# Attention tiles two at a time between the first layer's products, a later first weight step in slab 8, later residual sums

## The chip, the cores and the metric

The kernel runs on one core of a Trainium2 chip. The time is the device time of one execution in microseconds (us), the median of several runs. The profile is that of one execution.

## What is computed

A chain of three layers over 4608 rows (8 batches of 576) of width 512, all in float32:

```python
# 1. attention in chunks of 64 rows, 8 heads of 64
scores = scale * np.matmul(q_c, k_c.transpose(0, 1, 2, 4, 3))
attn = np.exp(scores - np.max(scores, axis=-1, keepdims=True))
attn = attn / (np.sum(attn, axis=-1, keepdims=True) + 1e-09)
x = np.matmul(attn, v_c)          # then heads side by side: 4608 x 512
# 2. first layer, 512 -> 2048 -> 512, with a residual
xn = (x - mu) / np.sqrt(var + 1e-06) * g_ln
x = x + np.maximum(xn @ w_ch1, 0.0) @ w_ch2
# 3. second layer, 512 -> 1024 -> 512, with a convolution of three taps as a gate
h = np.maximum(x @ w_in, 0.0)
return (h * sigmoid(conv(h, conv_w))) @ w_out
```

## The kernel before

Rows go in 36 attention tiles T of 128 rows (two chunks of 64) and in 9 slabs p of 512 rows (tiles 4p to 4p+3). Every large matmul is made of three matmuls (`mm3`, lines 113 to 115) on high and low parts of both operands; ScalarE makes the high part by a cast and VectorE the low part by a subtraction. PSUM is one tile, `banks`, of eight banks.

**Start.** A string, `START`, lists steps by letter and number. For the weights `w_ch1`, a block of four 128x512 pieces: `W` load, `a` (ScalarE), `t`, `m`, `n` (VectorE) turn raw bits into float32, `g` (ScalarE) scales, `s` (VectorE) makes sums, `h` (ScalarE) and `l` (VectorE) make the two parts. The number is that of a piece (0 to 15), for `h` and `l` that of an operand of the products (0 to 27). The letters of attention are below. What stands behind the `|` is run slot by slot in slab 0.

**First layer, first half.** `xn @ w_ch1` is done by the seven products of a fast 2x2 block scheme. A *slot* is one product, 12 matmuls of 128x256 (`product(p, G, n)`). A slab has 4 groups G of 7 slots s, so slot number 28p + 7G + s. `SLOTS` gives the product n of each s, and a lag of one group for two of them. Products 1, 6, 7 and 4 of a group pile up in one bank (4 or 5 by G), and ScalarE copies the running sum out (`u1`, `u6`, `u7`, `u4`, lines 605 and 614) before the next is added. Products 5 and 3 pile up in another bank and product 2 has its own; VectorE adds them to the copies (`plus`, line 159), and SyncE's queue stores the sum in `hd`. At G = 3 the operands of the next slab are made (`both`: a cast on ScalarE into `xc`, line 502, a subtraction on VectorE, line 156).

**Attention, put between slots.** `session(t, tv)` puts the work of tile tv behind slots t to t+4, together with the first half of the next tile, ts = tv+1:
- `V` (TensorE, line 380): 16 matmuls on 64x64 of the array, weights times values, of tv; `S` (same line): 16 such for the scores of ts. Each is two records in the trace (x32).
- `M` (VectorE, 396 and 397): maximum over scores; `X` (VectorE, 434): divide; `L`: loads of q, k, v for the tile after next.
- `E` (ScalarE, 406): 8 exponentials of a tile, in two halves; `R` (VectorE): reciprocals; `B`, `x` (VectorE): normalization of rows.
- `P` (TensorE, 420), `T` (TensorE, 462): four transposes each, of the exponentials of ts and of the rows of tv; `C` and `e` (ScalarE, 426 and 468): copies out of them, to `pt` (which the next `V` reads) and `bst` (from which the next slab's operands come).

Attention uses banks 0 and 1 for `S` and `V`, 0 for `P`, 3 for `T`.

**Slab 8.** It has no sessions. At slot (G, s) = (0, 5) the pool of attention is given back, and loads follow in SyncE's queue: three of `hr` (512 KB of `hd` each) and two raw pieces of `w_ch2` (`wd`). `cv_step` moves the preparation of `w_ch2` one step on: `h` of one piece, `a` of another on ScalarE, `m` and `l` on VectorE, one more load. ScalarE runs its queue in order, so an `a` whose load is out holds the copies behind it.

**First layer, second half.** `Down`: for each slab 16 blocks f of 12 matmuls of 128x512, summed in four banks (0 to 3 and 4 to 7 by turns). `split` makes a block's operands one block ahead: `hh` on ScalarE (685), `hl` on VectorE (686). After a slab's last block, `finish` adds the four sums to the rows of x (`xr`, four additions on VectorE, line 159).

**Second layer.** `Gate` and `outtile`; the change doesn't touch them.

Each engine takes its instructions in the order of the program text, with waits on semaphores between engines.

Of the kernel before, what the change touches and what calls it, by code (L numbers as in the profile page):

```python
# [23 lines left out]
h7 B2 e1 B3 h6 u1 l7 v1 y3 l8 z3 s4 e3 y2 s6 z2 s5 e2 l6 h11 j0 u2 j1 u3  # L24
s7 u5 v3 u7 h10 l11 j2 l10 u6 v2 h12 v6 j3 l12 u4 v5 h13 v4 l13 v7
|
S4 M4 E4 a8 t8 a10 t10 m8 n8
/ g8 a9 t9 m10 n10
/ g10 a11 a12 t11 t12 m9 R4 P4
/ C4 a14 n9 t14 g9 m12  # L30
/ h14 n12 m11 g12 n11 a13
/ l14 t13 g11 m14 h15
/ n14 s8 g14 l15 a15
/ h16 t15 s9 m13 l16 n13
/ s10 g13 s11 h21 h17
# [9 lines left out]
def attn_moe_moe2(  # L45
# [30 lines left out]
    N0, _, D, _, HP = q0.shape[:5]  # L76
    NTILE = N0 + q.shape[0]
# [4 lines left out]
    NS = NT // 512  # L82
# [75 lines left out]
    def plus(out, a, b):  # L158
        nc.vector.tensor_tensor(out=out, in0=a, in1=b, op=ALU.add)  # L159
# [182 lines left out]
    class Attention:  # L342
# [13 lines left out]
        def tile(self, shape, tag, bufs):  # L356
            return self.p.tile(shape, F32, tag=tag, bufs=bufs, name=tag)

        def L(self, T):
            for nm, to in (("q", self.q), ("k", self.k)):  # L360
                t = self.tile([128, HP * 2 * 64], "r" + nm, 2)
                if T < N0:
                    src = (q0 if nm == "q" else k0)[T].rearrange("c d e j s -> e d c (j s)")
                    for e in range(2):
                        nc.sync.dma_start(
                            out=t[half(e)].rearrange("p (c n) -> p c n", c=2), in_=src[e]
                        )
                    to[T] = t.rearrange("p (c j s) -> p j c s", c=2, s=64)
                else:
                    src = (q if nm == "q" else k)[T - N0]  # L370
                    nc.sync.dma_start(out=t, in_=src.rearrange("e p j c s -> (e p) (j c s)"))
                    to[T] = t.rearrange("p (j c s) -> p j c s", c=2, s=64)
            t = self.tile([128, HP * 2 * 64], "rv", 3)
            nc.sync.dma_start(out=t, in_=v[T].rearrange("e s j c d -> (e s) (j c d)"))
            self.v[T] = t.rearrange("p (j c d) -> p j c d", c=2, d=64)
# [22 lines left out]

        def E(self, T, js=range(4)):
            if T not in self.pp:  # L400
                self.sm[T] = self.tile([128, 2, HP], "sm", 3)
# [116 lines left out]
    with tc.manual_schedule():  # L518
# [4 lines left out]
        at = Attention()  # L523
# [15 lines left out]
        def one(step):  # L539
            kind, i = step[0], int(step[1:])  # L540
            if kind in "atmng":
                getattr(blocks[i // 4], kind)(i % 4)
            elif kind == "W":
                blocks[i // 4].W(i % 4, nc.sync)
            elif kind == "w":
                blocks[i // 4].W(i % 4, nc.scalar)
            elif kind == "s":
                blocks[i // 4].s(i % 4)
            elif kind in "hl":
                getattr(blocks[i // 7], kind)(i % 7)  # L550
            elif kind in "juv":
                getattr(slabs[0], kind)(i)
            elif kind == "S":
                at.S(i, (4, 6, 0, 4, 0)[i])
            elif kind == "V":
                at.V(i, (4, 6, 0, 4)[i])
            elif kind == "P":
                at.P(i, 0 if i > 3 else 2)
# [20 lines left out]
        def product(p, G, n):  # L579


            to = {1: 4 + G % 2, 6: 4 + G % 2, 7: 4 + G % 2, 4: 4 + G % 2, 5: 6 + G % 2, 3: 6 + G % 2, 2: 2}[n]
            x = slabs[p].xc[n]
            for i in range(2):
                f = 2 * G + i
# [10 lines left out]
            def flat(t):  # L596
                return t.rearrange("p a n -> p (a n)")
# [8 lines left out]
            if n == 7:  # L606

                t = tops.pop((p, G, 7))
                plus(flat(t), bank[6 + G % 2], flat(t))
                store(3, t)  # L610
            if n == 4:

# [11 lines left out]
                plus(flat(t), bank[to], flat(t))  # L624
                store(1, t)

        SLOTS = ((1, 0), (5, 0), (4, 1), (6, 0), (3, 1), (2, 0), (7, 0))
        events = {}

        def on(t, fn):  # L630
            events.setdefault(t, []).append(fn)

        def session(t, tv):

            ts = tv + 1 if tv + 1 < NTILE else None

            def begin():
                at.V(tv)
                if ts is not None:
                    at.S(ts)  # L640
                    at.M(ts)
                at.X(tv)
                if tv + 2 < NTILE:
                    at.L(tv + 2)

            on(t, begin)
            if ts is not None:
                on(t + 1, lambda: at.E(ts, (0, 1)))
                on(t + 2, lambda: at.E(ts, (2, 3)))
            on(t + 1, lambda: at.B(tv))  # L650
            on(t + 2, lambda: at.x(tv))

            if tv % 4 == 3:
                on(t + 3, lambda: (at.T(tv), at.e(tv)))
            if ts is not None:
                on(t + 4, lambda: (at.R(ts), at.P(ts)))
            if tv % 4 != 3:
                on(t + 4, lambda: at.T(tv))
            if ts is not None:
                on(t + 4, lambda: at.C(ts))  # L660
            if tv % 4 != 3:
                on(t + 4, lambda: at.e(tv))

        for tv in range(4, NTILE):

            t = 28 * (tv // 4 - 1) + 7 * (tv % 4 - 1) + 1
            session({4: 5, 5: 9, 6: 13, 7: 17}.get(tv, t), tv)

        class Down:

# [30 lines left out]
        for p in range(NS + 1):  # L701
            if p + 1 < NS:
                slabs[p + 1] = Slab(p + 1)
            for G in range(4):
                for s, (n, lag) in enumerate(SLOTS):
# [15 lines left out]
                    if p == NS - 1:  # L721
# [9 lines left out]
                        elif (G, s) == (2, 5):  # L731
                            tags = [f"w0{kk}{i}" for kk in range(2) for i in range(7)]
                            for f, tag in zip(F_ORDER[EARLY:], tags):
                                add_w2(f, lambda: wa_p, tag)
                            cv_load(NF1)
                        elif (0, 5) < (G, s) < (2, 5) and s % 2 == 0 or (G, s) in ((3, 1), (3, 3), (3, 5)):
                            cv_step()
                        if (G, s) == (3, 4):
                            parts = down.split(0)
# [51 lines left out]
        todo = [(p, f) for p in range(NS) for f in F_ORDER]  # L791
        downs = {0: down}
        xrs = {}
        for n, (p, f) in enumerate(todo):
            hh, hl = parts

# [7 lines left out]
                parts = downs[todo[n + 1][0]].split(todo[n + 1][1])  # L804
            if p == 0 and n % 4 < 3 or n % 2:
                cv_step()
            if f == 4:
                xrs[p] = residual(downs[p])
            if late and f >= 8:
                late.pop(0)()  # L810
            downs[p].down(f, hh, hl)
            if f == NF1 - 1:
                finish(downs[p], xrs[p])
            if (p, f) == (0, 15):
                cv_rest()
                load_cw()
# [195 lines left out]
```

## Time and profile before

| | |
|---|---|
| median of 3 runs | 1308.42 us (1308.25 to 1308.7) |
| the profiled execution | 1309.48 us, of which the span of its instructions is 1307.5 us |
| TensorE busy | 1249.2 us, 96% |
| VectorE, ScalarE busy | 748.9 us (57%), 614.8 us (47%) |

Times in the rows below are us from the span's start. TensorE's rows overlap, since a matmul's record lasts until its result is out; the pace of TensorE is the distance from start to start. The granted clock of TensorE (PEclk) is a share of 2.4 GHz: 1.00, or 0.50, which is 1.2 GHz, or a mean of both.

### The profile page before, as it was taken

To read this page: it belongs to the slowest core of one execution; us is meant where nothing else is said; L and a number is where in the kernel's file an instruction comes from. 1 tells how busy PE (TensorE), PEld (TensorE's weight loads), DVE (VectorE), ACT (ScalarE), POOL (GpSimd) and SP (SyncE) were. 2 spreads that over 40 slices of the span, in tenths; PEclk is the share of its full clock that TensorE was granted. 3 is DMA by queue.
4 is the path that set the end of the run, shared out by engine and by line. 5 is a ranking of instruction groups with operands and counts; after the bars stand their busy time and mean duration, and the time that the engine had idled before them with its cause. 6 is when DMAs were issued, how large, how long until landed. Compare 5 with 4: busy or idle time off the path is not lost.

```text
span 1307.5 us, 23314 instructions
## 1 busy us (share of the span) xinstructions
PE 1249.2 (96%) x9096; PEld 1087.0 (83%) x9096; DVE 748.9 (57%) x1430; ACT 614.8 (47%) x1510; POOL 76.2 (6%) x172
## 2 busy tenths in 40 slices
PE   5559999999999989999999999999999999999998
PEld 4459999999999978787788888888788888888887
DVE  7986565566556557667733443343876655565540
ACT  6765555556556435343322222222765555455541
POOL 0000000000000000000000000000121211111100
PEclk6689999999999989999999999999999999999999
DMA  9534555555455358486444355432111111101001
GB/s 267 169 106 170 186 172 168 188 186 177 168 183 191 114 205 298 146 296 211 145 153 161 128 178 178 161 130 81 33 57 58 43 37 57 57 28 53 25 25 49
DMA packets 127021, 177.70 MB, mean 136 GB/s; under 512 B 12736, under 2 KB 72128, under 8 KB 126912
## 3 DMA queue, kind: packets, MB, share of 16 engines
q1 hardware_dynamic: 126912, 176.22, 40.3%
q8 instruction: 71, 1.16, 0.4%
q14 instruction: 38, 0.31, 0.1%
HBM read 110.13 MB, written 66.06 MB: 135 GB/s over the span
## 4 chain that ended last, share of the span: by engine, by line
PE 85%; DVE 6%; ACT 4%; DMA 3%; issue 1%; SPq 1%; POOL 0%; DVEq 0%; ACTq 0%; POOLq 0%
PE banks L113 27%; PE banks L114 26%; PE banks L115 26%; PE banks L380 3%; PE banks L462 1%; PE banks L420 1%; DMA w<-in_moe_w_ch_dram 1%; DVE w L156 1%; ACT pp L406 1%; DMA wd<-in_moe_w_ch_dram 1%; DVE w L151 0%; DMA x2d<-x2T 0%; ACT w L335 0%; DVE xr L159 0%; DVE w L145 0%
## 5 line engine op out<-in xcount | busy, mean ns | idle before, releaser
L113 PE MATMUL banks<-xc,w 128*128 128x256 f32 x1008 | 290.4, 288 | 7.6 <-ACT u L605 7.1
L114 PE MATMUL banks<-xc,w 128*128 128x256 f32 x1008 | 283.2, 281 | 4.5 <-DVE xc L156 4.5
L115 PE MATMUL banks<-xc,w 128*128 128x256 f32 x1008 | 282.9, 281 | 0.0
L685 ACT ACTIVATE hh<-hr 128x512 fp32r<-128x512 f32 x144 | 91.1, 632 | 262.0 <-PE banks L115 261.8
L686 DVE SCALAR_TENSOR_TENSOR hl<-hr,hh 128x512 fp32r<-128x512 f32 x144 | 99.2, 690 | 192.1 <-ACT hh L685 189.9
L113 PEld LDWEIGHTS banks<-xc,w 128*128 128x128 f32 x1008 | 193.3, 192 | 10.5 <-ACT u L605 7.5
L114 PEld LDWEIGHTS banks<-xc,w 128*128 128x128 f32 x1008 | 193.6, 192 | 4.7 <-DVE xc L156 4.7
L115 PEld LDWEIGHTS banks<-xc,w 128*128 128x128 f32 x1008 | 193.3, 192 | 0.0
L113 PE MATMUL banks<-w,hl 128*128 128x512 f32 x396 | 154.7, 391 | 0.0
L114 PE MATMUL banks<-w,hh 128*128 128x512 f32 x396 | 154.1, 389 | 0.0
L115 PE MATMUL banks<-w,hh 128*128 128x512 f32 x396 | 154.1, 389 | 0.0
L896 DVE SCALAR_TENSOR_TENSOR cv<-hb,cw_sb,cv 128x510 f32<-128x510 f32 (+31 forms) x256 | 117.2, 512 | 0.6
L113 PE MATMUL banks<-xb,w 128*128 128x512 f32 x288 | 113.5, 394 | 1.8 <-ACT hb L881 1.4
L114 PE MATMUL banks<-xb,w 128*128 128x512 f32 x288 | 113.0, 393 | 0.0
L115 PE MATMUL banks<-xb,w 128*128 128x512 f32 x288 | 112.9, 392 | 0.0
L159 DVE TENSOR_TENSOR u<-banks,u 128x512 f32<-128x512 f32 x108 | 73.6, 688 | 56.2 <-ACT u L605 31.1
L406 ACT ACTIVATE pp<-banks,mx 128x64 f32<-128x64 f32 x288 | 87.8, 336 | 8.1 <-DVE mx L397 5.4
L605 ACT COPY u<-banks 128x512 f32<-128x512 f32 x108 | 64.0, 593 | 56.7 <-PE banks L115 54.1
L113 PEld LDWEIGHTS banks<-w,hl 128*128 128x128 f32 x396 | 74.3, 188 | 17.4 <-DVE hl L686 2.1
L115 PEld LDWEIGHTS banks<-w,hh 128*128 128x128 f32 x396 | 74.3, 188 | 15.6
L114 PEld LDWEIGHTS banks<-w,hh 128*128 128x128 f32 x396 | 74.3, 188 | 15.2
L883 POOL COPY hal<-hb 128x2 f32<-128x2 f32 x64 | 41.8, 652 | 736.6 <-ACT hb L881 736.6
(106 smaller groups left out, 2197.8 us busy)
## 6 DMA issues: line engine op xcount, KB each, us to landing
hd<-u SPq DMA_DIRECT2D x144, 256.0 KB, 2.9
hr<-hd SPq DMA_DIRECT2D x72, 512.0 KB, 3.8
w<-in_moe_w_ch_dram SPq DMA_DIRECT2D x27, 512.0 KB, 6.8
rv<-in_v_dram SPq DMA_DIRECT2D x36, 256.0 KB, 3.7
xd<-x SPq DMA_DIRECT2D x36, 256.0 KB, 2.0
xr<-xd SPq DMA_DIRECT2D x36, 256.0 KB, 4.3
x2d<-x2T SPq DMA_DIRECT2D x36, 256.0 KB, 2.0
x2r<-x2d SPq DMA_DIRECT2D x36, 256.0 KB, 4.0
```

The lines of the kernel that those rows point to most:

```text
L113: nc.tensor.matmul(ps, ll, rh, start=first, stop=False, **kw)
L114: nc.tensor.matmul(ps, lh, rl, start=False, stop=False, **kw)
L115: nc.tensor.matmul(ps, lh, rh, start=False, stop=last, **kw)
L156: nc.vector.tensor_tensor(out=out, in0=a, in1=b, op=ALU.subtract)
L159: nc.vector.tensor_tensor(out=out, in0=a, in1=b, op=ALU.add)
L380: nc.tensor.matmul(ps[half(c), e, j, :], lt[half(e), j, c, :], rt[half(e), j, c, :], start=True, stop=True,)
L406: nc.scalar.activation(out=pp[:, j, e, :], in_=self.both[T][:, e, j, :], func=AF.Exp, scale=SCALE, bias=mx[:, e, j:j + 1], accum_out=sm[:, ...
L605: nc.scalar.copy(flat(t), bank[to])
L685: nc.scalar.activation(out=self.hh, in_=t, func=AF.Relu)
L686: nc.vector.scalar_tensor_tensor(out=self.hl, in0=t, scalar=0.0, in1=self.hh.bitcast(F32), op0=ALU.max, op1=ALU.subtract,)
L883: nc.gpsimd.tensor_copy(out=hal[:, f, :], in_=hb[:, 512:514])
L896: nc.vector.scalar_tensor_tensor(out=cv[:, a:e], in0=hb[:, a + tap:e + tap], scalar=cw_sb[:, tap, f:f + 1], in1=cv[:, a:e], op0=ALU.mult, ...
```

## The change

A session now takes two tiles (tv, tv+1), each with banks of its own (0 and 1, or 2 and 3: `side`). Behind slot t stand `V` `V` `S` `S`, and behind slot t+6 (`turn`) `P` `P` `T` `T`. A slab has two sessions, at its slots 0 and 13, in place of four. Products 5 and 3 use bank 6 in all groups, product 2 uses bank 7, and `SLOTS` takes the products in another order. In slab 0, the sessions of tiles 4 to 7 are at slots 7 and 14 in place of 5, 9, 13 and 17. In slab 8, `cv_step` is not run at (0, 6), so the first is that of (1, 0). `finish` runs one block later, behind the next `split`.

```diff
-S4 M4 E4 a8 t8 a10 t10 m8 n8
-/ g8 a9 t9 m10 n10
-/ g10 a11 a12 t11 t12 m9 R4 P4
...
+S4 S5 M4 M5 E4 L6 L7 a8 t8 a10 t10 m8 n8
+/ E5 g8 a9 t9 m10 n10
+/ g10 a11 a12 t11 t12 m9
...
-            to = {1: 4 + G % 2, 6: 4 + G % 2, 7: 4 + G % 2, 4: 4 + G % 2, 5: 6 + G % 2, 3: 6 + G % 2, 2: 2}[n]
+            to = {1: 4 + G % 2, 6: 4 + G % 2, 7: 4 + G % 2, 4: 4 + G % 2, 5: 6, 3: 6, 2: 7}[n]
...
-        SLOTS = ((1, 0), (5, 0), (4, 1), (6, 0), (3, 1), (2, 0), (7, 0))
+        SLOTS = ((1, 0), (2, 0), (3, 1), (6, 0), (4, 1), (5, 0), (7, 0))
...
-            ts = tv + 1 if tv + 1 < NTILE else None
+            tvs = tv, tv + 1
+            tss = [T for T in (tv + 2, tv + 3) if T < NTILE]
+            side = lambda T: T % 2 * 2
 
             def begin():
-                at.V(tv)
-                if ts is not None:
-                    at.S(ts)
-                    at.M(ts)
-                at.X(tv)
-                if tv + 2 < NTILE:
-                    at.L(tv + 2)
+                for T in tvs:
+                    at.V(T, side(T))
+                for T in tss:
+                    at.S(T, side(T))
+                for i in range(2):
+                    if tss:
+                        at.M(tss[i])
+                    at.X(tvs[i])
...
+            def turn():
+                for T in tss:
+                    at.R(T)
+                    at.P(T, side(T))
+                for T in tvs:
+                    at.T(T, side(T) + 1)
+                for i in range(2):
+                    at.e(tvs[i])
+                    if tss:
+                        at.C(tss[i])
 
             on(t, begin)
...
+            for i, T in enumerate(tss):
+                on(t + 1 + 2 * i, lambda T=T: at.E(T, (0, 1)))
+                on(t + 2 + 2 * i, lambda T=T: at.E(T, (2, 3)))
+            for i, T in enumerate(tvs):
+                on(t + 1 + i, lambda T=T: at.B(T))
+                on(t + 3 + i, lambda T=T: at.x(T))
+            on(t + 6, turn)
...
-        for tv in range(4, NTILE):
+        for tv in range(4, NTILE, 2):
...
-            t = 28 * (tv // 4 - 1) + 7 * (tv % 4 - 1) + 1
-            session({4: 5, 5: 9, 6: 13, 7: 17}.get(tv, t), tv)
+            t = 28 * (tv // 4 - 1) + (13 if tv % 4 else 0)
+            session({4: 7, 6: 14}.get(tv, t), tv)
...
-                        elif (0, 5) < (G, s) < (2, 5) and s % 2 == 0 or (G, s) in ((3, 1), (3, 3), (3, 5)):
+                        elif (0, 6) < (G, s) < (2, 5) and s % 2 == 0 or (G, s) in ((3, 1), (3, 3), (3, 5)):
...
+            if ended is not None:
+                finish(downs[ended], xrs[ended])
+                ended = None
...
             downs[p].down(f, hh, hl)
             if f == NF1 - 1:
-                finish(downs[p], xrs[p])
+                ended = p
```

**TensorE at a session** in slab 1 (`rv,pt` is `V`, `rk,rq` is `S`; the rows around are products). Before:

```order
L115 MATMUL banks<-xc,w_679 128x256
L380 MATMUL banks<-rv,pt 64x64 x16
L380 MATMUL banks<-rk,rq 64x64 x16
L113 MATMUL banks<-xc,w_931 128x256
L114 MATMUL banks<-xc,w_931 128x256
```

The same place with the change:

```order
L115 MATMUL banks<-xc,w_620 128x256
L384 MATMUL banks<-rv,pt 64x64 x32
L384 MATMUL banks<-rk,rq 64x64 x32
L113 MATMUL banks<-xc,w_340 128x256
L114 MATMUL banks<-xc,w_340 128x256
```

Each group has doubled, and there are half as many groups.

**ScalarE at a session** at the turn of two slabs (`pp` exponentials, `u` copies of running sums, `xc` casts for the next slab, `bst` and `pt` the copies `e` and `C`). Before, for one tile:

```order
L605 COPY u1_4332<-banks_171 128x512
L502 CAST xc_4337<-bst_3768 128x512
L502 CAST xc_4353<-t1_4334 128x512
L614 COPY u4_4412<-banks_171 128x512
L406 ACTIVATE pp_4416,sm_4415<-banks_171,mx_4388 128x64 x4
L605 COPY u6_4440<-banks_171 128x512
L502 CAST xc_4442<-bst_3768 128x512
L406 ACTIVATE pp_4416,sm_4415<-banks_171,mx_4388 128x64 x4
L502 CAST xc_4479<-bst_3768 128x512
L426 COPY pt_4493<-banks_171 128x512
```

With the change, for two tiles at slot 0 of a slab:

```order
L611 COPY u1_3769<-banks_171 128x512
L410 ACTIVATE pp_3874,sm_3873<-banks_171,mx_3835 128x64 x4
L506 CAST xc_3900<-bst_3281 128x512
L410 ACTIVATE pp_3874,sm_3873<-banks_171,mx_3835 128x64 x4
L611 COPY u6_3926<-banks_171 128x512
L410 ACTIVATE pp_3929,sm_3928<-banks_171,mx_3841 128x64 x4
L620 COPY u4_3948<-banks_171 128x512
L506 CAST xc_3951<-bst_3281 128x512
L410 ACTIVATE pp_3929,sm_3928<-banks_171,mx_3841 128x64 x4
L611 COPY u7_3984<-banks_171 128x512
L472 COPY bst_4008<-banks_171 128x4x128
L430 COPY pt_4010<-banks_171 128x512
```

Sixteen exponentials stand between the copies where eight stood.

**ScalarE in slab 8** (`cy<-wd` is `a` of a piece of `w_ch2`, which waits for its load). Before:

```order
L605 COPY u7_6686<-banks_171 128x512
L133 ACTIVATE cy_6690<-wd0_6670 128x512
L605 COPY u1_6706<-banks_171 128x512
L133 ACTIVATE cy_6708<-wd1_6672 128x512
L614 COPY u4_6739<-banks_171 128x512
```

With the change:

```order
L611 COPY u7_6686<-banks_171 128x512
L611 COPY u1_6702<-banks_171 128x512
L133 ACTIVATE cy_6704<-wd0_6670 128x512
L133 ACTIVATE cy_6736<-wd1_6672 128x512
L611 COPY u6_6755<-banks_171 128x512
L620 COPY u4_6769<-banks_171 128x512
```

The copy `u1` has moved ahead of the first piece; `u6` is the first one behind the pieces, and two pieces stand ahead of it.

## Rows read from the trace of the kernel before

**Rows 1.** Waits of TensorE, whole span: for whom, us in total, times, longest.
```profile
PE banks L380 <- ACT pt L426: 14.5, 6, 5.7
PE banks L113 <- ACT u L605: 7.1, 2, 6.5
PE banks L113 <- DVE hl L686: 3.4, 3, 1.4
```
**Rows 2.** Stretches: length; busy PE, PEld, DVE, ACT, POOL; PEclk, DMA, GB/s.
```profile
65.50:104.80 39.30, 26.04 (x335) 24.48 (x330) 30.86 (x61) 23.04 (x68) 1.94 (x2) 0.78 0.36 115
127.00:450.00 323.00, 322.94 (x4219) 317.03 (x4218) 188.83 (x398) 178.09 (x627) 14.81 (x27) 1.00 0.51 174
450.00:506.00 56.00, 48.41 (x407) 47.78 (x406) 29.69 (x50) 23.96 (x43) 0.00 (x0) 0.94 0.64 229
```
**Rows 3.** Order of time, TensorE at a session: start, us, engine, line, operands, count.
```profile
224.47 0.28 PE L115 MATMUL banks<-xc,w 128*128 128x256 f32 x1
224.68 0.69 PE L380 MATMUL banks<-rv,pt 64*64 64x64 f32 x32
225.19 0.65 PE L380 MATMUL banks<-rk,rq 64*64 64x64 f32 x32
...
226.11 0.28 PE L115 MATMUL banks<-xc,w 128*128 128x256 f32 x1
```
**Rows 4.** Order of time, TensorE at the last session, which has V alone.
```profile
437.00 0.28 PE L115 MATMUL banks<-xc,w 128*128 128x256 f32 x1
437.21 0.69 PE L380 MATMUL banks<-rv,pt 64*64 64x64 f32 x32
...
438.17 0.28 PE L115 MATMUL banks<-xc,w 128*128 128x256 f32 x1
```
**Rows 5.** Order of time, TensorE: transposes P and T between products.
```profile
231.22 0.28 PE L115 MATMUL banks<-xc,w 128*128 128x256 f32 x1
231.33 0.60 PE L420 MATMUL banks<-ident,pp 128*128 128x128 f32 x4
231.77 0.60 PE L462 MATMUL banks<-ident,xn 128*128 128x128 f32 x4
...
232.32 0.28 PE L114 MATMUL banks<-xc,w 128*128 128x256 f32 x1
```
**Rows 6.** Order of time, ScalarE: exponentials and a copy of a running sum.
```profile
229.33 0.33 ACT L406 ACTIVATE pp<-banks,mx 128x64 f32<-128x64 f32 x1
229.53 0.22 ACT L406 ACTIVATION_READ_ACCUMULATOR pp<-banks,mx 128x1 f32 x1
229.62 0.60 ACT L605 COPY u<-banks 128x512 f32<-128x512 f32 x1
230.09 0.36 ACT L406 ACTIVATE pp<-banks,mx 128x64 f32<-128x64 f32 x1
```
**Rows 7.** Order of time, VectorE: M and X of a session.
```profile
225.91 0.69 DVE L396 TENSOR_REDUCE mx<-banks 128x8 f32<-128x512 f32 x1 [1.93 <-PE banks L380]
226.71 0.69 DVE L434 TENSOR_TENSOR x<-banks,sm 128x512 f32<-128x512 f32 x1
```
**Rows 8.** Waits of VectorE between 65.5 and 104.8 us.
```profile
DVE mx L396 <- PE banks L380: 5.2, 2, 3.5
DVE w L156 <- ACT w L335: 2.5, 4, 0.7
```
**Rows 9.** Order of time, TensorE: slot 14 of slab 0, and slot 27.
```profile
99.60 0.58 PE L113 MATMUL banks<-xc,w 128*128 128x256 f32 x1
...
125.45 0.37 PE L113 MATMUL banks<-xc,w 128*128 128x256 f32 x1
```
**Rows 10.** Order of time, slab 8: SyncE's queue, ScalarE, and TensorE behind it.
```profile
466.35 1.19 SPq L124 DMA_DIRECT2D wd<-in_moe_w_ch_dram  x2
...
473.88 0.69 ACT L133 ACTIVATE cy<-wd 128x512 f32<-128x512 f32 x1 [8.71 <-DMA wd<-in_moe_w_ch_dram]
...
475.10 0.58 PE L113 MATMUL banks<-xc,w 128*128 128x256 f32 x1 [6.46 <-ACT u L605]
```

More of the change, by code (lines that the diff above doesn't have):

```diff
@@ L26 @@
 |
-S4 M4 E4 a8 t8 a10 t10 m8 n8
-/ g8 a9 t9 m10 n10
-/ g10 a11 a12 t11 t12 m9 R4 P4
-/ C4 a14 n9 t14 g9 m12
-/ h14 n12 m11 g12 n11 a13
-/ l14 t13 g11 m14 h15
+S4 S5 M4 M5 E4 L6 L7 a8 t8 a10 t10 m8 n8
+/ E5 g8 a9 t9 m10 n10
+/ g10 a11 a12 t11 t12 m9
+/ a14 n9 t14 g9 m12
+/ R4 P4 C4 h14 n12 m11 g12 n11 a13
+/ R5 P5 C5 l14 t13 g11 m14 h15
 / n14 s8 g14 l15 a15
@@ L357, in tile, with L @@
             return self.p.tile(shape, F32, tag=tag, bufs=bufs, name=tag)
-        def L(self, T):
+        def L(self, T, late=False):
             for nm, to in (("q", self.q), ("k", self.k)):
@@ L372, in L, with Lv @@
                     to[T] = t.rearrange("p (j c s) -> p j c s", c=2, s=64)
+            if not late:
+                self.Lv(T)
+        def Lv(self, T):
             t = self.tile([128, HP * 2 * 64], "rv", 3)
@@ L400, in E @@
             if T not in self.pp:
-                self.sm[T] = self.tile([128, 2, HP], "sm", 3)
+                self.sm[T] = self.tile([128, 2, HP], "sm", 4)
                 self.pp[T] = self.tile([128, HP, 2, 64], "pp", 2)
@@ L553, in one @@
             elif kind == "S":
-                at.S(i, (4, 6, 0, 4, 0)[i])
+                at.S(i, (4, 6, 0, 4, 0, 2)[i])
             elif kind == "V":
@@ L557, in one @@
             elif kind == "P":
-                at.P(i, 0 if i > 3 else 2)
+                at.P(i, i % 2 * 2 if i > 3 else 2)
+            elif kind == "L":
+                at.L(i, late=i > 5)
             elif kind in "y":
@@ L608, in product @@
                 t = tops.pop((p, G, 7))
-                plus(flat(t), bank[6 + G % 2], flat(t))
+                plus(flat(t), bank[6], flat(t))
                 store(3, t)
@@ L633, in session @@
         def session(t, tv):
-            ts = tv + 1 if tv + 1 < NTILE else None
+            tvs = tv, tv + 1
+            tss = [T for T in (tv + 2, tv + 3) if T < NTILE]
+            side = lambda T: T % 2 * 2
             def begin():
-                at.V(tv)
-                if ts is not None:
-                    at.S(ts)
-                    at.M(ts)
-                at.X(tv)
-                if tv + 2 < NTILE:
-                    at.L(tv + 2)
-            on(t, begin)
-            if ts is not None:
-                on(t + 1, lambda: at.E(ts, (0, 1)))
-                on(t + 2, lambda: at.E(ts, (2, 3)))
@@ L650, in session @@
[L650 to L662, printed above, removed]
-        for tv in range(4, NTILE):
-            t = 28 * (tv // 4 - 1) + 7 * (tv % 4 - 1) + 1
-            session({4: 5, 5: 9, 6: 13, 7: 17}.get(tv, t), tv)
+                for T in tvs:
+                    at.V(T, side(T))
@@ new lines, in begin @@
+                for T in tss:
[5 more added lines that the diff above has]
+                for T in tss:
+                    if T + 2 < NTILE:
+                        at.L(T + 2, late=True)
+                for T in tss:
+                    at.Lv(T)
+            def turn():
+                for T in tss:
+                    at.R(T)
[6 more added lines that the diff above has]
+                        at.C(tss[i])
@@ L806, in attn_moe_moe2 @@
                 cv_step()
+            if ended is not None:
+                finish(downs[ended], xrs[ended])
+                ended = None
             if f == 4:
@@ L830, in attn_moe_moe2 @@
         cv_rest()
+        finish(downs[NS - 1], xrs[NS - 1])
         for fn in late:
```

## The prediction

> **What bounds the kernel now.** I read the page first: TensorE is busy for 1249.2 of 1307.5 us, so a gain must come either out of its 58 us of idle time or out of work that it does. Then its waits [rows 1]: 14.5 us for `pt`, the copy that `V` reads, 7.1 us for a copy `u` of a running sum, of which 6.5 are one wait, and 3.4 us in three waits for `hl`. Then stretches [rows 2]: in the steady part (127 to 450 us) TensorE has no idle time worth a word, VectorE and ScalarE are busy 58% and 55%, and the granted clock is 1.00. So there only less work on TensorE shortens it. In slab 0 (65.5 to 104.8 us) VectorE is the busiest, 30.9 of 39.3 us, and TensorE is granted 0.78. From 450 to 506 us 7.6 us are idle and 0.94 is granted.
>
> **Term 1: half as many groups of 64x64 matmuls.** The pace of products: from the third matmul of a run at 226.11 to its 48th at 231.22 [rows 3, 5] are 45 steps, 0.1136 us each, so a slot is 1.36 us. Around `V S`, from the last product (224.47) to the third one behind (226.11), 1.64 us pass; three steps of these are 0.34, so `V S` costs 1.30 us [rows 3]. Around `V` alone it is 1.17 - 0.34 = 0.83 us [rows 4]. `S` by itself is then worth 0.47, `V` taken as equal, and the remaining 0.36 us are paid for each entry into such a group. `V V S S` should cost 0.36 + 4 x 0.47 = 2.24 us where two groups cost 2.60. From slot 28 on there are 27 groups before (26 `V S`, one `V`) and 14 with the change: 13 x 0.36 = 4.7 us. Tile 8's `V` and `T` move from slab 0 into this stretch and cost 0.47 + 0.44 there, so 3.8 us stay. Transposes pay no entry: from 231.22 to 232.32 less two steps are 0.87, and one set is 0.44 from start to start [rows 5], so that `P P T T` is no cheaper than twice `P T`. Ends: 0 less the 0.9 if the entry belongs to each tile's banks and not to the group, and 5.
>
> On that entry the Trainium skill has a rule: TensorEngine Tiling (Array Packing), Key Properties, says that a change of tiling mode drains the engine, and TensorE: Matmul & The Clock Gate, step 4 (drain) of its step-by-step part, puts a drain at some 128 cycles, 0.05 us at 2.4 GHz. By my estimate from these pages two changes make 0.11 us an entry and 1.4 us in all in place of 4.7; the rows show three times as much, and the sum keeps to the rows.
>
> **Term 1's cover: ScalarE and VectorE in a session of two tiles.** I follow the tighter one, at slot 0 of a slab, from the start of that slot's product. It ends at 1.4, `V V S S` at 3.6, and slots 1 to 6 end at 5.0, 6.4, 7.7, 9.1, 10.4, 11.8. The first scores are out at 3.1; `M` takes 0.80, so exponentials start at 4.0. They follow each other by 0.29 us, and a copy takes 0.47 of the queue [rows 6]. ScalarE: four to 5.2; a cast that must wait for the product of slot 2 (6.5), to 7.0; four to 8.2; `u6` to 8.7; four to 9.9; `u4` to 10.4; a cast to 10.9; four to 12.1. The last transposes of the second tile are due at 12.6: 0.5 us to spare. VectorE: `M X M X` (0.80 and 0.69 each) [rows 7] to 6.1, `B` to 7.2, the additions of products 2 and 3 to 8.4; product 5 shares bank 6 and needs the latter at 9.1: 0.7 us to spare. Product 6 needs `u1`, 7 needs `u6`, and each stands two slots behind its copy. In the session at slot 13 no casts fall in. So the steady part gets no new wait, on a thin cover: without it each of 13 sessions would wait.
>
> **Term 2: the start, slots 0 to 27.** VectorE's chain from `n12` to the last weight step `l27` ends at 104.8 us, with 7.7 us of waits in it [rows 8], 5.2 of them for scores: `M6` and `M7` stand behind `V5` and `V6`, which wait for `C5` and `C6` in ScalarE's queue. With sessions at 7 and 14 both copies have several slots. The new chain lacks `M5`, `X6` and one addition (0.8 + 0.7 + 0.6) and has one more pair of reciprocals (0.4), so 29.2 us of work for 30.9; it begins 0.7 later, since one addition now comes in slot 1. Of the waits I keep 2.3 (one for `u7`, whose product waits for `u6` behind `E5` on ScalarE, and those of `l24`, `l26`, `l27` for their casts) and 0.5 of small gaps. The chain then ends at 65.5 + 0.7 + 29.2 + 2.8 = 98.2. On ScalarE `h24`, some 5 us before that end, stands ahead of `h25`, `u7`, `e4`, `C6`, `e5`, `C7`: seven steps of 0.5 us to 96.7. `V7 S8 S9` follow (1.6 us with the way out), so slot 15 starts at 98.3; before it started at 99.60 + 12 x 0.213 = 102.2 (1.2 GHz) [rows 9]. From there to slot 28 the new order has 13 slots (17.7) and one `P P T T` (1.8); 7 us at 1.2 GHz behind the wait, of which the stretch before had some 17 (0.22 of 39.3 us, doubled), lose 3.4. Slot 28 at 121.2, where it was at 125.45 + 1.4 = 126.9 [rows 9]: 5.7 us. Ends: 0, if VectorE's idle time only goes elsewhere, and 10, if these waits and the low clock go too. A session now puts eight transfers in a row into SyncE's queue where there were four; the stores of sums behind them are due when their buffer is written again, two groups (19 us) later, so I cost this at nothing.
>
> **Term 3: slab 8.** `a` of the first piece of `w_ch2` starts when its load lands, at 473.88, and holds `u1` of slot (1, 0); product 6 at (1, 3) waits 6.46 us for it [rows 10]. Now `u1` stands ahead. The first copy held is `u6` of (1, 3), and product 7 at (1, 6) needs it: three slots or 4.1 us on. Two pieces stand ahead of it instead of one, worth 0.6 (ScalarE's own time) to 1.5; the loads leave some 0.5 earlier, because the store of slot (0, 5), which stood ahead of them in SyncE's queue, now comes earlier. Wait: 6.46 - 4.1 + 1.0 - 0.5 = 2.9 us, a gain of 3.6. The clock in this stretch, 0.94 of 56 us [rows 2], means some 6.7 us at 1.2 GHz; if a shorter wait avoids that, 1.5 more, and if it falls just at the restart, 2 less. I take 3.5, ends 1.5 and 5.
>
> **Term 4: `finish`.** The four additions stand ahead of `hl` of the next slab's second block, and three slab ends wait for it [rows 1], 1.4 us at most: two of 1.4 and one of 0.6. With `split` first, `hl` no longer waits for the additions, and the next `hl` has a block of 2.7 us to come. The shortest, at the end of slab 0, stays: there the convolution weights' load and steps now stand ahead of it in either order, and the additions behind may push the next `hl` by 0.3. So 2.5, ends 2.2 and 3.4.
>
> **The sum.** 3.8 + 5.7 + 3.5 + 2.5 = 15.5 us off the profiled execution's 1309.48 is 1294.0; that execution stood 1.06 above the median, so the median should be **1292.9**.
>
> **Rivals.**
> - *The start gives nothing.* For it: VectorE is the busiest there, and the same weight steps stand in the same slots. Against it: 7.7 us of its waits. 1292.9 + 5.7 = 1298.6.
> - *The entry goes with each tile*, since the pair of banks changes inside a group. The rows show no group of two tiles in the steady part. 1292.9 + 4.7 = 1297.6.
> - *Slab 8's wait only moves*, since it ends with the loads: 1292.9 + 3.5 = 1296.4.
> - *ScalarE is late in each session*, the other side. If the exponentials' records, 0.33 and 0.22 us [rows 6], did not overlap, four would take 2.2 us, the sixteenth would end at 15.1, and the last transposes would wait 2.5 us; in 13 sessions that is some 30 us: 1323. It decides from 15.5 / 13 = 1.2 us a session. Against it: their starts stand 0.29 apart. In this direction points TensorEngine Tiling (Array Packing), PSUM Bottleneck, in the Trainium skill: array tiling speeds up TensorE but not the way out of PSUM, which may become the bound; the steady part, with ScalarE at 55%, does not show it, but it has one tile a session.
>
> **Chances.** My forecast 0.50, no gain at the start 0.20, entry by tile 0.10, slab 8 0.10, both better ends at the start and in slab 8 (about 1287) 0.05, ScalarE late 0.05. No measurement of this kernel can tell a change under 0.2% (2.6 us) from none. Two of the smaller losses together still end near 1303. Range 1283 to 1304, the likeliest case alone 1288 to 1297; faster 0.90, same 0.04, slower 0.06.
>
> **What would show it.** Right: `V` and `S` at 2.2 to 2.3 us for a group of four; no wait of TensorE between 130 and 450 us; waits for `pt` well under 14.5 us; slot 28 near 121 us; in slab 8 a wait of about 3 us for `u`; one short wait for `hl`. Wrong: waits of `P` for exponentials or of products for `u` in every session, or slot 28 near 127.

## The result, and the profile after

| | before | after |
|---|---|---|
| median | 1308.56 us (4 runs, 1308.25 to 1314.1) | 1292.13 us (4 runs, 1290.76 to 1294.0) |
| ratio, with its 95% interval | | 0.9864 (0.9851 to 0.9877) |
| the profiled execution, its span | 1309.48, 1307.5 us | 1292.32, 1290.5 us |
| TensorE busy | 1249.2 us | 1239.9 us |

The change made the kernel 16.4 us faster by the medians; 15.5 were forecast, and the time on record was 1292.9. Where the 17.0 us between the two spans come from, by the start of the first matmul of each stretch:

| stretch | predicted | in the traces |
|---|---|---|
| the span's start to slot 28 (126.91; after 120.80) | 5.7 | 6.1 |
| slot 28 to slot 224, the start of slab 8 (to 454.87; to 444.14) | 3.8 | 4.6 |
| slab 8, to the first matmul of `Down` (to 505.70; to 490.58) | 3.5 | 4.4 |
| `Down`, to the first matmul of `Gate` (to 903.25; to 886.29) | 2.5 | 1.8 |
| `Gate` to the end | 0 | 0.01 |

The waits of TensorE over the whole span (for whom, us in total, times, longest), which answer to [rows 1]:

```profile
PE banks L384 <- DMA rk<-in_k_dram: 14.9, 4, 8.8
PE banks L113 <- DVE u L159: 8.1, 3, 5.4
PE banks L384 <- ACT pt L430: 7.0, 3, 3.7
...
PE banks L113 <- ACT u L611: 3.0, 2, 2.1
...
PE banks L113 <- DVE hl L702: 0.6, 2, 0.5
```

The waits for `pt` fell from 14.5 to 7.0 us, for `u` from ScalarE from 7.1 to 3.0, for `hl` from 3.4 to 0.6. Two rows are larger. The one for loads of a `k` grew from 5.6 to 14.9 us, mainly by one wait of 8.8 us behind slot 0. The one for additions on VectorE grew from 0.4 to 8.1 us: one wait of 5.4 us in slab 0, at 84 us, and two in slab 8.

Stretches, as in [rows 2] (length; busy PE, PEld, DVE, ACT, POOL; PEclk, DMA, GB/s): the 13 slots from 15 to 28, the steady part, and slab 8.

```profile
101.00:120.80 19.80, 19.80 (x176) 19.73 (x173) 14.75 (x32) 12.50 (x46) 1.26 (x2) 1.00 0.60 199
122.00:444.00 322.00, 322.00 (x4287) 318.52 (x4286) 188.39 (x405) 178.23 (x630) 16.60 (x28) 1.00 0.51 176
444.00:491.00 47.00, 42.21 (x365) 41.58 (x364) 27.52 (x45) 20.38 (x36) 0.00 (x0) 1.00 0.76 274
```

In the steady part TensorE has no idle time, as before; VectorE and ScalarE stay at 59% and 55%. In slab 8 the granted clock is now 1.00 all through, where it was 0.94.

TensorE at a two-tile session and at its transposes, in order of time, as in [rows 3, 5]:

```profile
190.83 0.28 PE L115 MATMUL banks<-xc,w 128*128 128x256 f32 x1
191.03 1.16 PE L384 MATMUL banks<-rv,pt 64*64 64x64 f32 x64
192.01 1.11 PE L384 MATMUL banks<-rk,rq 64*64 64x64 f32 x64
...
193.40 0.28 PE L115 MATMUL banks<-xc,w 128*128 128x256 f32 x1
...
201.23 0.28 PE L115 MATMUL banks<-xc,w 128*128 128x256 f32 x1
201.34 1.04 PE L424 MATMUL banks<-ident,pp 128*128 128x128 f32 x8
202.22 1.04 PE L466 MATMUL banks<-ident,xn 128*128 128x128 f32 x8
...
203.33 0.28 PE L115 MATMUL banks<-xc,w 128*128 128x256 f32 x1
```

From 190.83 to 193.40 less three steps of 0.113 us are 2.23 us for `V V S S` (all 13 such groups: 2.23 to 2.24), for which the prediction had 2.24; two groups `V S` of before are 2.60. `P P T T` takes 2.10 less three steps, 1.76, where twice `P T` of before is 1.78 (median): transposes save nothing by it, as said.

The start, as in [rows 9] (TensorE: `V V` behind slot 14, slot 15, slot 28; VectorE: a maximum over scores, and the last weight step; ScalarE: the copy `C7`):

```profile
97.59 2.10 PE L384 MATMUL banks<-rv,pt 64*64 64x64 f32 x64 [3.67 <-ACT pt L430]
...
100.99 0.39 PE L113 MATMUL banks<-xc,w 128*128 128x256 f32 x1
...
120.80 0.28 PE L113 MATMUL banks<-xc,w 128*128 128x256 f32 x1
...
59.76 0.69 DVE L400 TENSOR_REDUCE mx<-banks 128x8 f32<-128x512 f32 x1 [3.38 <-PE banks L384]
...
100.55 0.69 DVE L156 TENSOR_TENSOR w<-s,w 128x512 fp32r<-128x512 f32 x1 [0.68 <-ACT w L335]
...
97.89 0.62 ACT L430 COPY pt<-banks 128x512 f32<-128x512 f32 x1
```

Slot 28 starts at 120.80 us, 121.2 were forecast. But slot 15 starts at 100.99 and not at 98.3, and the last weight step ends at 101.2 and not at 98.2; a second error, of the other sign, makes up for that (below).

Slab 8, as in [rows 10]: SyncE's queue, ScalarE, and TensorE at slots (1, 0) and (1, 6) and at its two later waits:

```profile
453.66 0.28 PE L113 MATMUL banks<-xc,w 128*128 128x256 f32 x1
...
454.15 0.61 SPq L124 DMA_DIRECT2D wd<-in_moe_w_ch_dram  x1
...
461.57 0.69 ACT L133 ACTIVATE cy<-wd 128x512 f32<-128x512 f32 x1 [5.77 <-DMA wd<-in_moe_w_ch_dram]
...
464.04 0.39 PE L113 MATMUL banks<-xc,w 128*128 128x256 f32 x1 [2.06 <-ACT u L611]
...
473.61 0.39 PE L113 MATMUL banks<-xc,w 128*128 128x256 f32 x1 [1.13 <-DVE u L159]
...
487.74 0.39 PE L113 MATMUL banks<-xc,w 128*128 128x256 f32 x1 [1.60 <-DVE u L159]
```

The wait stands where it was forecast, at product 7 of (1, 6), and is 2.06 us for the 2.9 predicted. All waits of TensorE in slab 8 are 4.79 us here; before they were 7.59 (6.46, 0.68 and 0.45). That is 2.8 of the 4.4 us. The other 1.6 are left for the low clock: before, 0.65 was granted from 475 to 480 us.

### The profile page after: what moved, and what is told of

The parts are those of the page before. It is cut to its first block, busy times and chain, and to the rows that moved or that the text cites. A ratio compares the mean times of both kernels' runs of the same rounds, so it can differ in the third digit from the quotient of the medians.

```text
span 1290.5 us, 23238 instructions
## 1 busy us (share of the span) xinstructions
PE 1239.9 (96%) x9096; PEld 1080.4 (84%) x9096; DVE 744.1 (58%) x1430; ACT 613.9 (48%) x1510; POOL 78.0 (6%) x172
## 4 chain that ended last, share of the span: by engine, by line
PE 84%; DVE 6%; DMA 5%; ACT 3%; SPq 1%; issue 1%; ACTq 0%; DVEq 0%
PE banks L113 27%; PE banks L114 26%; PE banks L115 26%; PE banks L384 3%; DMA rk<-in_k_dram 1%; DMA w<-in_moe_w_ch_dram 1%; PE banks L466 1%; DVE w L156 1%; PE banks L424 1%; DMA wd<-in_moe_w_ch_dram 1%; DVE hl L702 1%; DMA x2d<-x2T 0%; DVE w L151 0%; DVE u L159 0%; DVE w L145 0%
## 5 line engine op out<-in xcount | busy, mean ns | idle before, releaser
L115 PEld LDWEIGHTS banks<-w,hh 128*128 128x128 f32 x396 | 74.3, 188 | 15.5
```

Source lines behind the costliest of these rows:

```text
L115: nc.tensor.matmul(ps, lh, rh, start=False, stop=last, **kw)
```

## The experiments

All times are medians. The runs were made in four groups, each on one chip with runs of before beside it (1308.86, 1308.9, 1308.76 and 1309.19 us). A kernel made from before is judged by its ratio; one made from the changed kernel by its median against 1292.13 and by its trace; the four medians of before lie within 0.5 us, so that the chips can be compared. The theory is that of the prediction: four gains in four places. Its rivals are that the entry into a group of 64x64 matmuls costs less than the rows say, that the start gives nothing, that slab 8's wait only moves, and that ScalarE is late.

**1. `finish` one block later, alone** (on the kernel before).

```diff
             if f == NF1 - 1:
-                finish(downs[p], xrs[p])
+                ended = p
```

(and `finish` of `ended` behind the next `split`.)

> The kernel before with the four residual additions one block later, nothing else. By the prediction's fourth term TensorE's three waits for hl at slab ends (3.4 us) shrink to one and the time falls by 2.5 us (2.2 to 3.4), to about 1306. The stretch from the first down matmul to the first gate matmul was 1.84 us shorter in the profile of the changed kernel while its waits fell by 2.7; if the other 0.8 us belongs to this edit, the time falls by 1.8 only. If hl only becomes late one block on, it falls by less than 0.7 us.

1306.02 us, ratio 0.9979 (0.997 to 0.9987): 2.7 us faster, 1.7 to 3.9. TensorE's waits for `hl` are now one, in this row, and `Down` takes 395.13 us where it took 397.55.

```profile
PE banks L113 <- DVE hl L686: 0.5, 1, 0.5
```

So term 4 has its size, 2.5; the 1.8 of the changed kernel's trace lies inside the interval too.

**2. Slab 8's first weight step at (1, 0), alone** (on the kernel before).

```diff
-                        elif (0, 5) < (G, s) < (2, 5) and s % 2 == 0 or (G, s) in ((3, 1), (3, 3), (3, 5)):
+                        elif (0, 6) < (G, s) < (2, 5) and s % 2 == 0 or (G, s) in ((3, 1), (3, 3), (3, 5)):
```

> The kernel before with the first weight step of slab 8 at slot (1, 0) instead of (0, 6), nothing else. By the prediction's third term the 6.46 us wait for a copy u becomes one of 2.9 us and the time falls by 3.5 us (1.5 to 5), to about 1305. In the changed kernel the stretch gained 4.4 us, with a wait of 2.06 us and no fall of the granted clock; if the edit alone brings that, the time is about 1304. If the wait only moves because it ends with the loads, the time stays within 1 us of before.

1307.87 us, ratio 0.9995 (0.9986 to 1.0004): 0.7 us faster, at most 1.8, where 3.5 were forecast. SyncE's queue, ScalarE and TensorE at (1, 6), in order of time:

```profile
465.89 1.25 SPq L124 DMA_DIRECT2D wd<-in_moe_w_ch_dram  x2
...
474.48 0.67 ACT L133 ACTIVATE cy<-wd 128x512 f32<-128x512 f32 x1 [8.40 <-DMA wd<-in_moe_w_ch_dram]
...
476.94 0.58 PE L113 MATMUL banks<-xc,w 128*128 128x256 f32 x1 [4.69 <-ACT u L605]
```

Slot (1, 0) starts at 463.93 here. The loads are issued 1.96 us behind it, and the first `a` comes 10.55 us behind it; in the changed kernel these are 0.49 and 7.91. Of these 2.64 us, 1.47 are the issue, and 1.17 the way of the load: the first piece lands 8.6 us behind its issue here, 7.4 in the changed kernel and 7.5 in before. The wait is 4.69 us, and the row behind it lasts 0.58 us: the granted clock fell again, to 0.52 from 475 to 480 us. What sets the time of issue in the changed kernel's slab 8 is the order of the products.

**3. The order of the products in slab 8, with the step and without it** (on the kernel before).

```diff
+        LAST = ((1, 0), (2, 0), (3, 1), (6, 0), (4, 1), (5, 0), (7, 0))
...
-                for s, (n, lag) in enumerate(SLOTS):
+                for s, (n, lag) in enumerate(SLOTS if p < NS - 1 else LAST):
```

> The kernel before with the first weight step of slab 8 at (1, 0), and in slab 8 alone the products in the order of the changed kernel (1, 2, 3, 6, 4, 5, 7). The step alone shortened the stretch from slot 224 to the first down matmul only from 50.8 to 49.9 us; in the changed kernel it is 46.4. There the first loads of slab 8 are issued 0.5 us behind the start of slot (1, 0), and 2.0 us behind it in the old order, in which the store of slot (0, 5) stands ahead of them. If that order makes the rest, the stretch is 46 to 47 us here and the time about 1304.5. If the rest comes from the sessions or from the end of slab 7, the stretch stays near 50 us and the time near 1308.

> The kernel before with, in slab 8 alone, the products in the order of the changed kernel, and the first weight step left at (0, 6). It is the fourth corner beside before (1308.8 us), the step alone (b_slab8, 1 us less) and both (b_slab8_order, 3.9 us less). If each edit had its own gain, the order alone gives 3 us, about 1306. If the order only brings the loads 1.5 us forward and the step still holds the copy u1, TensorE waits some 4.6 us as in a_slab8_old, the granted clock still falls behind it, and the time is within 1.5 us of before.

With the step: 1304.9 us, ratio 0.9973 (0.9964 to 0.9983), 3.5 us faster. Without it: 1308.04, ratio 0.9995 (0.9985 to 1.0004), 0.7. Each alone gives nothing that can be told from zero; both together give by the median what was forecast for the step. The profiled execution of the first was its slowest of 9 (1306.73), and it shows only half of this: its slab 8 takes 49.08 us, 1.75 less than before, where 46 to 47 were expected and the changed kernel takes 46.44. The rest of the 3.5 us is shown by the times alone. TensorE behind the wait in both, first with the step, then without it with the stretch around it:

```profile
474.98 0.58 PE L113 MATMUL banks<-xc,w 128*128 128x256 f32 x1 [3.42 <-ACT u L605]
```

```profile
473.82 0.58 PE L113 MATMUL banks<-xc,w 128*128 128x256 f32 x1 [4.85 <-ACT u L605]
...
470.00:480.00 10.00, 6.18 (x38) 6.18 (x39) 6.79 (x12) 5.04 (x9) 0.00 (x0) 0.66 0.94 334
```

In the old order the store of slot (0, 5), product 2, stands just ahead of the loads in SyncE's queue; in the new one the last store ahead is that of slot (0, 4). That brings the loads 1.5 us forward, in both runs to 0.50 us behind slot (1, 0). But as long as `a` at (0, 6) holds `u1`, a wait of 4.85 us is left, and behind it TensorE is granted 0.66 on average from 470 to 480 us. With the step the wait is 3.42 and not the changed kernel's 2.06, since the first piece lands 8.75 us behind its issue and not 7.4. In this run and in run 2, and in none of the other traces of this slab, a transfer of 16 KB in the queue of instructions, 1.1 us long, falls into that flight; that it makes the landing late was not tested.

**4. The changed kernel without the step**: `(0, 5)` again in that line.

> The changed kernel with the first weight step of slab 8 back at (0, 6). Its a then holds the copy u1 of (1, 0) until the load lands, some 7.9 us behind the start of (1, 0), and product 6 at (1, 3) waits for it: some 5 us instead of the 2.1 us at (1, 6). By the prediction's third term the time rises by 3.5 us, by the two traces by 4.4, to 1295.6 to 1296.5, and more if the clock falls behind the wait. If the order of the products made nearly all of the gain in slab 8, the time rises by 1 us or less.

1296.68 us, 4.6 more than with it. TensorE at (1, 3) and the stretch around it:

```profile
463.87 0.58 PE L113 MATMUL banks<-xc,w 128*128 128x256 f32 x1 [4.59 <-ACT u L611]
...
460.00:470.00 10.00, 6.13 (x35) 6.14 (x36) 6.74 (x12) 4.81 (x9) 0.00 (x0) 0.66 0.96 344
```

So in the new order the step is worth 4.6 us. In the traces slab 8 is 5.2 us longer: 1.7 of it are waits (2.5 at this one, 0.8 less at the later two), some 1.2 the slower pace of products that run 9 shows and that comes without this edit too, and the rest is the low clock behind the wait.

**5. `V V` one slot ahead of `S S`** (on the changed kernel).

```diff
-            on(t, begin)
+            on(t - 1, values)
+            on(t, begin)
```

(`values` holds the two `V`, the rest stays in `begin`.)

> The changed kernel with V V of a session one slot ahead of S S, so that each session pays two entries into groups of 64x64 matmuls instead of one; the same matmuls. If 0.36 us are paid for each entry into a group, 14 more entries cost 14 x 0.36 = 5.0 us and the time is about 1297; V V and S S then cost 0.36 + 2 x 0.47 = 1.30 us each. If the entry is some 0.11 us, as the estimate from the two pages would have it, they cost 1.05 each and the time rises by 1.5 us. If the cost belongs to the matmuls and not to the entry, nothing changes (1292).

1299.73 us, 7.6 more. Both groups of a session, with the products around them:

```profile
192.58 0.28 PE L115 MATMUL banks<-xc,w 128*128 128x256 f32 x1
192.79 1.16 PE L384 MATMUL banks<-rv,pt 64*64 64x64 f32 x64
...
194.22 0.28 PE L115 MATMUL banks<-xc,w 128*128 128x256 f32 x1
...
195.25 0.28 PE L115 MATMUL banks<-xc,w 128*128 128x256 f32 x1
195.46 1.16 PE L384 MATMUL banks<-rk,rq 64*64 64x64 f32 x64
...
196.89 0.28 PE L115 MATMUL banks<-xc,w 128*128 128x256 f32 x1
```

1.64 less 0.34 is 1.30 us for each, as expected: two groups of two take 2.60, one of four takes 2.23, and the same matmuls cost 0.37 more for each entry. From slot 28 to slot 224 the trace is 3.75 us longer, with one pair `V V` (1.3) less in it: 5.0, as forecast (13 more entries there make 4.8, a slightly slower pace the rest). The other 2.3 us lie ahead of slot 28: there `V` of tiles 4 to 7 stands one slot earlier and waits longer for `pt` (6.6 us in two waits, for 3.7 in one).

**6. Exponentials one slot later** (on the changed kernel).

```diff
-                on(t + 1 + 2 * i, lambda T=T: at.E(T, (0, 1)))
-                on(t + 2 + 2 * i, lambda T=T: at.E(T, (2, 3)))
+                on(t + 2 + 2 * i, lambda T=T: at.E(T, (0, 1)))
+                on(t + 3 + 2 * i, lambda T=T: at.E(T, (2, 3)))
```

> The changed kernel with the exponentials of a session one slot later (slots t+2 to t+5 instead of t+1 to t+4), the transposes still behind slot t+6; the same instructions. The last four exponentials then stand behind the copies of one more slot. By the working of the cover in the prediction (0.5 us to spare at slot 0 of a slab) the last ones end at about 13.8 us where they are due at 12.6: P waits 1.2 us in each session at slot 0 and less at slot 13, where no casts fall in: 7 x 1.2 + 7 x 0.4, some 11 us, and about 1303. If ScalarE has more to spare than worked out, no wait shows and the time stays at 1292.

1300.67 us, 8.5 more. `P P T T` takes 2.75 us at slot 0 of a slab (1.0 more) and 2.07 at slot 13 (0.3 more), in every one of 13 sessions; 7 x 1.0 + 6 x 0.3 = 8.8. TensorE at the first of them, whose second `P` waits, and `P` by all 13 (busy, mean ns; idle time before):

```profile
132.69 0.60 PE L424 MATMUL banks<-ident,pp 128*128 128x128 f32 x4
134.06 0.66 PE L424 MATMUL banks<-ident,pp 128*128 128x128 f32 x4 [0.77 <-ACT pp L410]
...
L424 PE MATMUL banks<-ident,pp 128*128 128x128 f32 x104 | 16.3, 280 | 5.6 <-ACT pp L410 5.2
```

The expectation was 1.2 and 0.4 a session: the cover is as thin as it was worked out, and the rival in which ScalarE is late has this price for one slot.

**7. The start of before** (on the changed kernel): the step list of before, and tiles 4 to 7 one at a time at slots 5, 9, 13 and 17, the last of which makes the scores of tiles 8 and 9.

```diff
-S4 S5 M4 M5 E4 L6 L7 a8 t8 a10 t10 m8 n8
+S4 M4 E4 a8 t8 a10 t10 m8 n8
...
+        for tv, t in ((4, 5), (5, 9), (6, 13), (7, 17)):
+            single(t, tv)
+
+        for tv in range(8, NTILE, 2):
```

> The changed kernel with the start of before: tiles 4 to 7 one at a time at slots 5, 9, 13 and 17, with the step list of before; the two-tile sessions begin at slot 28. If the gain up to slot 28 (6.1 us in the two traces, 5.7 in the prediction) comes from the sessions in the start and the steps beside them, slot 28 starts near 126.9 us again and the time is about 1298. If the new order of products and banks alone did it, the time stays at 1292.

In this run the transposes of tile 7 went into the bank that still held half of tile 9's scores, so that the rows of tile 9 are computed from other numbers. 1297.11 us, slot 28 at 127.88. The second one has them in bank 1:

> The changed kernel with the start of before, as a_start_old, but with the transposes of tile 7 in bank 1. Slot 28 is again expected near 127.9 us, 7.1 us later than in the changed kernel, and the time 5 to 7 us above it, near 1298. If bank 3 had made a wait in a_start_old, slot 28 comes earlier, and the start is worth less than that.

1296.18 us, 4.1 more than the changed kernel, and slot 28 at 126.01, 5.2 later:

```profile
126.01 0.28 PE L113 MATMUL banks<-xc,w 128*128 128x256 f32 x1
```

The start's part is worth 4 to 5 us; the rival in which it gives nothing falls.

**8. Earlier loads in the start** (on the changed kernel). SyncE's queue stands still from 28.5 to 37.7 us, because the store of tile 2's rows waits for `X2`; the loads of tile 5 are issued from 46.6 us on, behind three of 512 KB, and `S5` waits 8.8 us for its `k`.

```diff
-V1 B0 S2 X1 W8 W10
+V1 B0 S2 X1 W8 W10 W9 W11 L4
...
-E3 V2 l4 n7
+E3 V2 L5 W12 W14 W13 W15 l4 n7
...
-V3 X2 W9 W11 L4 W12 e0 l9 g4 z1 X3 W14 W13 W15 L5 h8
+V3 X2 e0 l9 g4 z1 X3 h8
```

> The changed kernel with the loads of tiles 4 and 5 and of the last six pieces of w_ch1 earlier in the queue of SyncE: ahead of the store of tile 2's rows, for which the queue stands still for some 9 us from 28.5 us on. The wait of S5 for its k in slot 0 (8.8 us) should be gone. If VectorE's wait for these scores (3.4 us) stands in the chain that ends at slot 15, slot 15 starts some 3 us earlier than 100.99 us and the time falls by 2.5 to 4 us, to about 1289. If that chain waits for something else anyway (ScalarE's casts of the weights), the time stays at 1292 and the wait comes back elsewhere in VectorE's queue.

1292.57 us, no gain. The 8.8 us are gone, and slot 15 starts at 99.85, 1.1 earlier; slot 28 at 120.36, 0.4 earlier. VectorE's waits from 45 to 101 us:

```profile
DVE w L156 <- ACT w L335: 2.8, 5, 0.7
DVE w L145 <- ACT w L133: 1.7, 1, 1.7
DVE u L159 <- ACT u L611: 1.4, 2, 1.1
```

Of the 3.4 us for scores, 1.7 come back as a wait for ScalarE's `a`. The longest wait of TensorE in the changed kernel held up next to nothing that sets the end.

**9. Slab 8's first step later still, at (1, 4)**, alone and with the loads of run 8.

```diff
-                        elif (0, 6) < (G, s) < (2, 5) and s % 2 == 0 or (G, s) in ((3, 1), (3, 3), (3, 5)):
+                        elif (1, 2) < (G, s) < (2, 5) and s % 2 == 0 or (G, s) in ((3, 1), (3, 3), (3, 5)):
```

> The changed kernel with the first weight step of slab 8 at slot (1, 4) instead of (1, 0). The copy u6 of (1, 3) then stands ahead of the first step that can wait for a load, so the 2.06 us wait at product 7 of (1, 6) should be gone and the time fall by about 2 us, to 1290. If the wait ends with the loads wherever the steps stand, it comes back at u7 of (1, 6) or later, and the time stays within 1 us of 1292; it rises if the steps that are missing by the first block of the second half make that block wait.

> The changed kernel with the earlier loads of a_loads and the first weight step of slab 8 at (1, 4). From the traces the start gives 0.4 us and slab 8 some 2.6 (the stretch to the first down matmul was 1.0 us shorter in a_slab8_14 although each of its 28 slots took 0.056 us more), so some 3 us: 1289, if the products run at 113 ns each in the steady part. If they run at 118 ns throughout, as they did in the profiled execution of a_slab8_14, the time is 7 to 9 us more, 1297 or so. If the wait of slab 8 only moves, it stays at 1292.

Alone: 1294.93 us, but six runs between 1291.18 and 1298.77, three of them under 1292.5 and three over 1297. With the loads: 1291.56 (1290.76 to 1292.32), 0.6 under the changed kernel, which no measurement here can tell from it. In the second, the wait of 2.06 us is gone, and two others stand further on:

```profile
471.56 0.39 PE L113 MATMUL banks<-xc,w 128*128 128x256 f32 x1 [0.83 <-ACT u L611]
...
485.81 0.38 PE L113 MATMUL banks<-xc,w 128*128 128x256 f32 x1 [3.05 <-DVE u L159]
```

The weight steps that came too early for the loads now pile up on VectorE ahead of an addition. At this end slab 8's wait does only move.

What may have split the first one's runs is seen in its profiled execution (1298.77 us), one of the three long ones; none of the short ones was profiled. TensorE in the steady part, two matmuls 36 apart, in the changed kernel and then in this run:

```profile
252.92 0.28 PE L114 MATMUL banks<-xc,w 128*128 128x256 f32 x1
...
257.00 0.28 PE L114 MATMUL banks<-xc,w 128*128 128x256 f32 x1
```

```profile
252.85 0.28 PE L115 MATMUL banks<-xc,w 128*128 128x256 f32 x1
...
257.09 0.28 PE L115 MATMUL banks<-xc,w 128*128 128x256 f32 x1
```

4.08 us are 0.1133 for each matmul, 4.24 are 0.1178. In this execution all 196 slots from 28 to 224 ran at the slower pace, 10.0 us in all over 113.4 ns a step; in the changed kernel's 25 did (1.4 us), in that of before 40 (2.4 us). The granted clock is 1.00 in all three. The stretch from slot 28 to slot 224 took 7.5 us more than in the changed kernel, with the same instructions.

## Why the prediction was right

**Term 1 (3.8).** Its prices held to 0.01 us: 2.23 for `V V S S` (2.24), 1.30 for a group of two, 0.37 for an entry (0.36), nothing for transposes. The stretch gave 4.6; 1.0 of that is the pace of the products just shown, and 3.6 is the term: 4.3 in groups of `V` and `S` (4.2 by the prediction), 0.7 saved in transposes, several of which came late before (a loss of 0.4 was forecast, for tile 8's `T`), and 1.4 lost, which the next paragraph names. So the mechanism and its price are right, but that the sum of the stretch came so near 3.8 is luck: the 1.1 that the transposes gave beyond the forecast nearly make up for the 1.4 lost. The rival in which the entry goes with each tile falls with the 2.23. The estimate from the Trainium skill's TensorEngine Tiling (Array Packing), Key Properties, and TensorE: Matmul & The Clock Gate, step 4, 0.11 us an entry, is shown wrong in size by run 5, where one entry more cost 0.37.

**Its cover.** TensorE has no wait from 122 to 444 us that the view of waits lists, and run 6 shows where the cover ends: one slot. But it was followed only at slot 0 of a slab. At G = 3, where VectorE also makes the next slab's operands, the addition of product 3 (slot 2) ends just as product 5 (slot 5), which now shares its bank, is due. TensorE around the start of that product in slab 1 of the changed kernel, then VectorE's addition:

```profile
164.41 0.28 PE L115 MATMUL banks<-xc,w 128*128 128x256 f32 x1
164.61 0.38 PE L113 MATMUL banks<-xc,w 128*128 128x256 f32 x1
164.84 0.28 PE L114 MATMUL banks<-xc,w 128*128 128x256 f32 x1
...
163.88 0.68 DVE L159 TENSOR_TENSOR u<-banks,u 128x512 f32<-128x512 f32 x1
```

The two steps of 0.20 and 0.22 us instead of 0.113 are 0.2 us lost; the same pause stands once in each of seven slabs, 1.4 us, and nowhere in the trace of before. That the shared bank makes it is read from these rows; no run gave product 5 a bank of its own. In the execution of run 9 that kept the slower pace, where product 5 comes later, the pause is missing.

**Term 2 (5.7; 6.1 in the traces, 4 to 5 by run 7).** The sum was right by two errors of opposite sign. The step "It begins 0.7 later" failed: the chain began with `n12` at 68.1 and not at 66.2. `S5` and its maximum had moved from slot 5 to slot 0, and the prediction did not follow their loads: the `k` of tile 5 lands at 58.0 us, and VectorE waited 3.4 us for the scores. Run 8, in which this `k` is early, has `n12` at 66.9, so 1.2 of the 1.9 us are the late `k`. VectorE's work was 28.8 us (29.2 counted), its waits and gaps 4.3 and not 2.8; so the chain ended 3.0 late. `C7`, which the `V` ahead of slot 15 needs, ended at 98.5 for 96.7, and from there to slot 15 it took 2.5 us for 1.6, with 0.72 granted from 95 to 101 us: slot 15 came 2.7 late. The other failed step is "7 us at 1.2 GHz behind the wait": from slot 15 to slot 28 the 13 slots ran at a granted 1.00 and took 19.8 us for the 22.9 forecast. The low clock lay ahead of slot 15.

**Term 3 (3.5; 4.4 in the traces).** The place was right, the cause only half. The mis-sized piece is "the loads leave some 0.5 earlier": they leave 1.5 earlier, by the new order of products. With 1.5 the prediction's own sum gives a wait of 1.9, and 2.06 was measured. Run 2 shows that without this order the step is worth 0.7 (the late landing there may have its share in that), and run 4 that without the step the order leaves a wait of 4.59. The "1.5 more" if the clock stays up came too (1.6), and the two waits for VectorE's additions, 1.13 and 1.60 us where 1.13 in all stood before, took as much back; the prediction had none there. The clock matters as much as the wait: it fell behind the waits of 3.4 to 4.9 us in the traces of runs 2 to 4, and not behind 2.06. In the faster executions of run 3 it may have stayed up: over a whole execution the mean granted clock was 0.971 in the profiled one, 0.973 in the median of the nine, and 0.971 in that of before beside them. But their times do not follow it, so this is not shown.

**Term 4 (2.5).** 2.7 by run 1.

What stays open: why a stretch of products runs at 118 ns a step and the next at 113, whether the shared bank makes the pause of 0.2 us, and why the trace of run 3 shows 1.75 us in slab 8 where its median gives 3.5.

## What to carry to other kernels

Price a group by what surrounds it: the difference between one group of four and two groups of two was read from the trace before at 0.36 us and held (0.37 in run 5), while an idle row of 8.8 us, the longest in the new profile, was worth nothing when it was removed. Two edits that look independent can each be worth too little alone to be told from zero and 3.5 us together, when one moves a load and the other the first instruction that waits for it; cost a later wait only after following what stands ahead of the load in its queue. And before an effect of a few us is read from two profiles, compare the pace of the steady part in both, since it made one steady part 7.5 us longer than another of the same instructions.

## What the hardware showed that was not expected

- Products of 128x256 run at one of two paces, 113 or 118 ns from start to start, at the same granted clock of 1.00, for stretches from a few slots to the whole steady part. In the traces of before and after the pace changes only where products start again, behind a group of transposes or 64x64 matmuls or behind the pause of 0.2 us just shown (5 of the 9 changes in the changed kernel's steady part are a step from 118 back to 113 behind a group, the 4 others one from 113 to 118 at that pause).
- Groups of 64x64 matmuls take the same time at either pace, 2.23 to 2.24 us for four sets.
- In slab 8 the granted clock fell to 1.2 GHz for some us behind waits of TensorE of 3.05, 3.42, 4.59, 4.69, 4.85 and 6.46 us, and stayed at 1.00 with waits of 1.13, 1.60, 2.06 and, in run 9, 2.83 us.
